# Where the operand and weight tiles of a float32r kernel begin in SBUF

## The chip, the core and the metric

The kernel runs on one core of a Trainium2 chip. The metric is the device time of one execution in microseconds. TensorE (PE in the profile; PEld is its weight load) multiplies; VectorE (DVE) and ScalarE (ACT) do the element work; GpSimd (POOL) and SyncE (SP) start transfers.

## The reference

Attention with a sigmoid in place of the softmax, then two feed-forward networks on its output, all in float32 precision at the end:

```python
scores = matmul(q, k.T) / sqrt(64) - log(448)      # 4 batches, 12 heads, 448 tokens, 64 wide
x = (1 / (1 + exp(-scores))) @ v                   # -> 1792 tokens x 768
h = x @ w_in;  x = maximum(h, 0) ** 2 @ w_out      # 768 -> 2048 -> 768
h = x @ w_in2; out = (h / (1 + exp(-1.702 * h))) @ w_out2
```

The weights come as 8-byte floats and are turned into float32 on the chip.

## The kernel before

**Precision.** TensorE multiplies float32r numbers, which are float32 rounded to fewer bits. For float32 results each operand is split: a high part, rounded to float32r by ScalarE, and a low part, which VectorE makes as the number less its high part. A product is then three matmuls into the same PSUM bank, high times high, high times low, low times high: lines 475, 476 and 477 in `product`. Each streams 448 columns of the operand past 128 × 128 weights, which PEld loads first.

**Tiling.** Each feed-forward matrix product is done in two halves of the tokens (`p`), and each half by a scheme of seven block products instead of eight (P1 to P7 on sums and differences of blocks). That makes 8 stages (`STAGES`) of 56 units (7 products by 8 strips); a unit has 3 chunks of 3 matmuls. 8 × 56 × 9 = 4032 matmuls, run in one fixed order. Attention comes before them, with matmuls of its own: lines 298 (float32r, 64 rows), 317, 332 and 346 (plain float32).

**Tiles that the change touches**, both in the pool `cpool`:

- `T` (line 101): five operand tiles of [128, 2, 3, 448] float32r, 10752 bytes in each partition. Index 0 of the second dimension is the high part, index 1 the low part, and the next index is k, the chunk of 128 rows of the contraction. The class `Operand` picks the tile that has been free longest; ScalarE writes `t[:, 0]` (helper line 153) and VectorE `t[:, 1]` (helper line 156).
- `SL` (line 103): three slots of weights, [128, 2, 2, 384] float32r, 6144 bytes; high and low part, two units, 3 chunks of 128 columns. Unit u uses slot u // 2 % 3. `plan_weights` fills them: SP loads the two units' blocks from DRAM (`scr`) into one of four `LD` tiles, ScalarE writes the high part, VectorE the low part, and TensorE waits for the latter (`lows`).

The pool places its tiles one after the other: X (four of 5376 bytes), T, LD (3072 bytes each), SL, `tmp`, RAW, DEC; after them comes a pool for attention, whose place four tiles for the hidden layer (h) and two of scratch (`sig`) take later. Ahead of all stand the scratch for GpSimd's transfers, 16384 bytes of each partition unless the program says otherwise, and four constants of 32 bytes' room each.

**Weights' way in.** `prep` (32 steps) moves a block of 8-byte floats with POOL's queue into `raw`, decodes it on ScalarE and VectorE into `dec`, makes four sums and differences, and stores blocks and sums with POOL's queue in `scr`. The 96 transfers of these steps are all that POOL starts.

**Order.** `settle` and `run` make a plan before the program is written: every operation is a node with a modelled duration, and a list scheduler orders the nodes of each engine by their latest starts. The plan knows tiles and their users, but no addresses. On the chip each engine runs its list in that order and waits on semaphores.

Of the kernel before, what the change touches and what calls it, by code (L numbers as in the profile page):

```python
# [9 lines left out]
F32R = mybir.dt.float32r  # L10
# [6 lines left out]
B, H, S, D = 4, 12, 448, 64  # L17
DM, DFF = 768, 2048
P = 128
# [10 lines left out]
NK = 3  # L30
NF = 8
W = NK * P
UNITS = 7 * NF
NLOAD = 4
NSLOT = 3
NT = 5
# [42 lines left out]

PACE = (6, 6, 5, 1, 4, 5, 5)  # L80


@with_exitstack
def sigmoid_attention_two_ffn(ctx: ExitStack, tc: tile.TileContext, qk, v, w, outT):
# [3 lines left out]
    nc = tc.nc  # L88
# [9 lines left out]

    cpool = ctx.enter_context(tc.tile_pool(name="cpool", bufs=1))
    X = [[cpool.tile([P, NK, S], F32, name=f"xq{i}{j}") for j in range(2)] for i in range(2)]  # L100
    T = [cpool.tile([P, 2, NK, S], F32R, name=f"t{n}") for n in range(NT)]
    LD = [cpool.tile([P, 2, W], F32, name=f"ld{n}") for n in range(NLOAD)]
    SL = [cpool.tile([P, 2, 2, W], F32R, name=f"s{n}") for n in range(NSLOT)]
    tmp = cpool.tile([P, NK, S], F32, name="tmp")
    RAW = [cpool.tile([P, 4 * W, 2], U32, name=f"raw{n}") for n in range(2)]
    DEC = [cpool.tile([P, 4, W], F32, name=f"dec{n}") for n in range(2)]
# [30 lines left out]
    def act(fn, n, keys=(), after=(), extra=0.0, **kw):  # L137
        return Node("act", fn, 0.115 + extra + 0.833e-3 * n, keys, after, 0.105, **kw)
# [4 lines left out]
    def move(eng, out, in_, size, keys=(), after=(), **kw):  # L143

        def go():
            eng.dma_start(out() if callable(out) else out, in_() if callable(in_) else in_)

        n = Node("sp" if eng is nc.sync else "pool", go, 0.45 if eng is nc.sync else 0.55, keys, after, DMA_US + size / 250e3, **kw)
        n.size = size
        return n  # L150

    def activation(out, in_, fn=AF.Copy, **kw):
        nc.scalar.activation(out, in_, fn, **kw)  # L153
# [9 lines left out]
    def att_order():  # L163
        for u in range(NHP // 2 + 1):
            if u:
                yield from (("V", hp, c) for hp in (2 * u - 2, 2 * u - 1) for c in range(NFULL))
                yield ("VL", u - 1, 0)
            if u < NHP // 2:
                todo = [("S", hp, c) for hp in (2 * u, 2 * u + 1) for c in range(NFULL)]
                todo.insert(0 if u else NFULL, ("SL", u, 0))  # L170
                yield from todo
# [3 lines left out]
    def make_steps():  # L175
        kind = "L"
        us = {"S": SCORES_US, "V": VALUES_US, "VL": LEFT_US, "SL": LEFT_US}
        for key in att_order():
            new = "L" if key[0] in ("VL", "SL") else key[0]
            t = us["V" if key in WHOLE else key[0]]  # L180
# [61 lines left out]
    def load_qk(hp):  # L242
        if hp > 1:
            n = move(nc.sync, RQ[hp % 4], qk[hp], P * 2 * S * 4, (), [pe.get(("SL", (hp - 4) // 2, 0)), split.get(hp - 4)], part=0)
            rq_load[hp] = n, n
# [29 lines left out]
    def next_two():  # L275
        turn[0] += 1
        b = 2 * (turn[0] % 4)
        return b, mem["ps"][:, b : b + 2]
# [28 lines left out]
    def scores_left(u):  # L307
        b, ps = next_two()
        step = pe["SL", u, 0]

# [90 lines left out]
    class Operand:  # L401

        def __init__(self, src, n, keys, first, last):
# [3 lines left out]
            free_t[i] = last  # L407
            self.t = t = T[i]
            keys = [("T", i), *keys]
            act(lambda: activation(t[:, 0, : src().shape[1]], src()), n * S, keys, [units[old]] if old >= 0 else ())  # L410
# [38 lines left out]
    def plan_weights():  # L449
        for q in range(len(STAGES) * UNITS // 2):  # L450
            m, io, _ = STAGES[2 * q // UNITS]
            us = [ORDER[io][(2 * q + i) % UNITS] for i in range(2)]
            t, sl = LD[q % NLOAD], SL[q % NSLOT]
            ld = ("LD", q % NLOAD)
# [414 lines left out]
```

## Time and profile before

| | us |
|---|---|
| median of 2 runs | 951.66 (951.35 to 951.98) |
| the profiled execution: its time | 950.77 |
| its span, first to last instruction | 949.0 |
| TensorE busy | 944.6 (x4949) |
| VectorE busy | 809.3 |
| ScalarE busy | 604.6 |
| GpSimd busy | 53.5 (x100) |

Busy time of TensorE counts matmuls that overlap in its pipeline, so it says that there was always one under way, and not at which rate they went. The step from one start to the next is read from the timeline or from a stretch and the number of its matmuls. Lines 153, 156 and 146 are helpers (`activation`, `tt`, `move`) through which most of ScalarE's and VectorE's work and all transfers of the plan go; their groups are told apart by the tiles' names.

### The profile page before, as it was taken

What the parts mean: (1) busy time and instruction counts of PE and PEld (TensorE: products, weight loads), DVE (VectorE), ACT (ScalarE), POOL (GpSimd) and SP (SyncE); (2) the same over time, 40 slices, a digit from 0 to 9 for tenths busy, and PEclk for the clock granted to TensorE, in tenths of its full rate; (3) what the DMA queues carried; (4) which work ended last, traced back from release to release, by engine and by line L of the source; (5) the groups of instructions that cost most, each with busy time, mean ns of one, the idle gap of its engine ahead of it and who ended that gap; (6) DMA issues with size and microseconds to landing.
All of it is one profiled execution on the core that took longest, in us unless ns stands there. A gap on an engine that the chain in (4) does not pass through costs nothing.

```text
span 949.0 us, 13696 instructions
## 1 busy us (share of the span) xinstructions
PE 944.6 (100%) x4949; PEld 822.8 (87%) x4949; DVE 809.3 (85%) x839; ACT 604.6 (64%) x715; POOL 53.5 (6%) x100
## 2 busy tenths in 40 slices
PE   9999999999999999999999999999999999999998
PEld 4555479999999999999999999999999999999997
DVE  3989986699877999999999987999989999778662
ACT  6788776778868775555464666657684646445551
POOL 0110100000000000000000000000000000000000
PEclk9999999999999999999999999999999999999999
DMA  8899989999886766896567699877975448754341
GB/s 340 301 335 356 335 293 332 324 354 334 290 324 227 250 231 212 317 364 216 161 243 286 202 359 325 312 247 251 351 279 171 133 146 288 261 166 132 115 137 58
DMA packets 98627, 245.75 MB, mean 259 GB/s; under 512 B 10752, under 2 KB 72960, under 8 KB 94464
## 3 DMA queue, kind: packets, MB, share of 16 engines
q1 hardware_dynamic: 84736, 150.51, 46.5%
q0 software_dynamic: 13824, 94.38, 27.2%
q8 instruction: 38, 0.62, 0.3%
q14 instruction: 29, 0.24, 0.1%
HBM read 175.11 MB, written 69.73 MB: 258 GB/s over the span
## 4 chain that ended last, share of the span: by engine, by line
PE 100%; ACT 0%; issue 0%
PE ps L475 29%; PE ps L476 29%; PE ps L477 29%; PE ps L332 6%; PE ps L298 5%; PE ps L346 1%; PE ps L317 1%; PE ps L790 0%; PE ps L293 0%; ACT xq L635 0%; PE ps L471 0%
## 5 line engine op out<-in xcount | busy, mean ns | idle before, releaser
L475 PE MATMUL ps<-t,s 128*128 128x448 f32 x1344 | 490.9, 365 | 0.0
L477 PE MATMUL ps<-t,s 128*128 128x448 f32 x1344 | 490.8, 365 | 0.0
L476 PE MATMUL ps<-t,s 128*128 128x448 f32 x1344 | 490.8, 365 | 0.0
L153 ACT ACTIVATE s<-ld 128x768 fp32r<-128x768 f32 x224 | 189.4, 846 | 249.4 <-PE ps L476 206.6
L477 PEld LDWEIGHTS ps<-t,s 128*128 128x128 f32 x1344 | 252.5, 188 | 19.9
L476 PEld LDWEIGHTS ps<-t,s 128*128 128x128 f32 x1344 | 252.5, 188 | 19.9
L475 PEld LDWEIGHTS ps<-t,s 128*128 128x128 f32 x1344 | 252.5, 188 | 19.9
L156 DVE TENSOR_TENSOR s<-ld,s 128x768 fp32r<-128x768 f32 x224 | 213.6, 954 | 61.7 <-ACT s L153 56.6
L156 DVE TENSOR_TENSOR t<-h,t 128x1344 fp32r<-128x1344 f32 (+1 forms) x72 | 100.4, 1397 | 8.8 <-ACT t L153 8.7
L153 ACT ACTIVATE t<-h 128x1344 fp32r<-128x1344 f32 (+1 forms) x72 | 85.6, 1190 | 4.4 <-DVE h L156 2.9
L153 ACT ACTIVATE h<-ps 128x448 f32<-128x448 f32 x112 | 59.8, 536 | 27.0 <-PE ps L477 26.8
L153 ACT ACTIVATE a<-ps,bias 128x896 f32<-128x896 f32 x72 | 66.1, 1023 | 3.2 <-PE ps L293 3.2
L332 PE MATMUL ps<-a,rv 128*64 128x448 f32 x288 | 56.8, 543 | 0.1
L217 DVE SCALAR_TENSOR_TENSOR dec<-raw,dec 128x1536 uint32<-128x1536 uint32 x32 | 56.2, 1755 | 0.5
L219 DVE SCALAR_TENSOR_TENSOR dec<-raw,dec 128x1536 uint32<-128x1536 uint32 x32 | 56.1, 1753 | 0.3
L153 ACT ACTIVATE dec<-raw 128x1536 f32<-128x1536 f32 x32 | 51.9, 1621 | 0.0
L156 DVE TENSOR_TENSOR h<-h,h 128x1344 f32<-128x1344 f32 (+1 forms) x36 | 50.0, 1397 | 1.0 <-DMA h<-hm 0.8
L153 ACT ACTIVATE h<-h 128x896 f32<-128x896 f32 x48 | 44.9, 945 | 4.8 <-DVE h L156 4.4
L332 PEld LDWEIGHTS ps<-a,rv 128*64 128x64 f32 x288 | 19.6, 137 | 32.4 <-issue 22.6
L213 DVE TENSOR_SCALAR dec<-dec 128x1536 f32<-128x1536 f32 x32 | 30.7, 959 | 15.6 <-ACT dec L153 15.6
L156 DVE TENSOR_TENSOR t<-xq,t 128x1344 fp32r<-128x1344 f32 x24 | 37.2, 1552 | 5.9 <-ACT t L153 5.4
L156 DVE TENSOR_TENSOR h<-ps,h 128x448 f32<-128x448 f32 x64 | 38.8, 619 | 2.8 <-PE ps L477 2.5
(58 smaller groups left out, 616.1 us busy)
## 6 DMA issues: line engine op xcount, KB each, us to landing
ld<-scr SPq DMA_DIRECT2D x448, 192.0 KB, 3.8
raw<-in_w POOLq DMA_DIRECT2D x32, 1536.0 KB, 8.2
scr<-dec POOLq DMA_DIRECT2D x32, 768.0 KB, 5.5
scr<-raw POOLq DMA_DIRECT2D x28, 576.0 KB, 6.2
hm<-h SPq DMA_DIRECT2D x32, 448.0 KB, 5.8
h<-hm SPq DMA_DIRECT2D x16, 672.0 KB, 5.4
rq<-in_qk SPq DMA_DIRECT2D x22, 448.0 KB, 8.2
rv<-in_v SPq DMA_DIRECT2D x12, 448.0 KB, 6.1
```

What stands on the lines that cost most here:

```text
L153: nc.scalar.activation(out, in_, fn, **kw)
L156: nc.vector.tensor_tensor(out=out, in0=in0, in1=in1, op=op)
L213: dve(lambda: nc.vector.tensor_scalar(out=d, in0=d, scalar1=LEAST, scalar2=LARGEST, op0=ALU.max, op1=ALU.min), 4 * W, [dk], each=0.52e-3)
L217: dve(lambda: nc.vector.scalar_tensor_tensor(out=u, in0=raw[:, :, 0], scalar=29, in1=u, op0=ALU.logical_shift_right, op1=ALU.bitwise_or), ...
L219: dve(lambda: nc.vector.scalar_tensor_tensor(out=u, in0=raw[:, :, 1], scalar=0x80000000, in1=u, op0=ALU.bitwise_and, op1=ALU.bitwise_or), ...
L298: nc.tensor.matmul(ps[:, j, :S], kk[rows, keys], qq[rows, QUERIES], start=(i == 0), stop=(i == 2))
L317: nc.tensor.matmul(ps[out, j, :S], r[rows, :LEFT], r[rows, QUERIES], start=True, stop=True)
L332: nc.tensor.matmul(ps[rows, :S], t[:, hp % 2 * NFULL + c, rows], a[:, j], start=(c == 0), stop=False)
L346: nc.tensor.matmul(mem["ps"][out, b + i, :S], t[rows, 2 * NFULL, out], AL[rows, j], start=False, stop=True)
L475: nc.tensor.matmul(o, sh[:, cols], t[:, 0, k], start=start, stop=False, skip_group_check=True)
L476: nc.tensor.matmul(o, sh[:, cols], t[:, 1, k], start=False, stop=False, skip_group_check=True)
L477: nc.tensor.matmul(o, lo[:, cols], t[:, 0, k], start=False, stop=stop, skip_group_check=True)
```

## The change

Each T tile grows from 10752 to 11264 bytes and each SL tile from 6144 to 6656, 512 bytes more, and the part that is used is cut out of the larger tile at an offset: 8, 10, 18, 20 and 24 elements of 4 bytes into T's tiles 0 to 4, and 0, 123 and 106 elements into the three slots. The shape that the rest of the kernel sees is as before. The scratch for GpSimd's transfers is set to 8192 bytes.

```diff
+SKIP_T, SKIP_SL = (8, 10, 18, 20, 24), (0, 123, 106)
...
-    T = [cpool.tile([P, 2, NK, S], F32R, name=f"t{n}") for n in range(NT)]
+    T = []
+    for n, skip in enumerate(SKIP_T):
+        t = cpool.tile([P, 2 * NK * S + P], F32R, name=f"t{n}")
+        T.append(t[:, skip : skip + 2 * NK * S].rearrange("p (a k n) -> p a k n", a=2, k=NK))
     LD = [cpool.tile([P, 2, W], F32, name=f"ld{n}") for n in range(NLOAD)]
-    SL = [cpool.tile([P, 2, 2, W], F32R, name=f"s{n}") for n in range(NSLOT)]
+    SL = []
+    for n, skip in enumerate(SKIP_SL):
+        t = cpool.tile([P, 4 * W + P], F32R, name=f"s{n}")
+        SL.append(t[:, skip : skip + 4 * W].rearrange("p (a i n) -> p a i n", a=2, i=2))
...
-    nc = bacc.Bacc("TRN2", target_bir_lowering=False, num_devices=1)
+    nc = bacc.Bacc("TRN2", target_bir_lowering=False, num_devices=1, dynamic_dma_scratch_size=8192)
```

## Rows read from the trace of the kernel before

**Rows 1.** The page's chain that ended last, shares by engine and line.

```profile
PE 100%; ACT 0%; issue 0%
PE ps L475 29%; PE ps L476 29%; PE ps L477 29%; PE ps L332 6%; PE ps L298 5%; PE ps L346 1%; PE ps L317 1%; PE ps L790 0%; PE ps L293 0%; ACT xq L635 0%; PE ps L471 0%
```

**Rows 2.** Stretch of the 4032 matmuls: its length, then busy us by engine.

```profile
core 0: us, PE busy (x) PEld busy (x) DVE busy (x) ACT busy (x) POOL busy (x), PEclk, DMA share, GB/s
128.22:945.41 817.19, 817.19 (x4032) 757.15 (x4031) 705.94 (x715) 501.66 (x603) 41.91 (x76) 1.00 0.72 248
```

**Rows 3.** Groups by line: names, shapes, count | busy us, mean ns | idle before.

```profile
L475 PE MATMUL ps<-t,s 128*128 128x448 f32 x1344 | 490.9, 365 | 0.0
L477 PE MATMUL ps<-t,s 128*128 128x448 f32 x1344 | 490.8, 365 | 0.0
L476 PE MATMUL ps<-t,s 128*128 128x448 f32 x1344 | 490.8, 365 | 0.0
L475 PEld LDWEIGHTS ps<-t,s 128*128 128x128 f32 x1344 | 252.5, 188 | 19.9
L476 PEld LDWEIGHTS ps<-t,s 128*128 128x128 f32 x1344 | 252.5, 188 | 19.9
L477 PEld LDWEIGHTS ps<-t,s 128*128 128x128 f32 x1344 | 252.5, 188 | 19.9
```

**Rows 4.** Timeline of TensorE from 300 us: start, us, engine, line.

```profile
300.00 0.37 PE L477 MATMUL ps<-t,s 128*128 128x448 f32 x1
300.20 0.36 PE L475 MATMUL ps<-t,s 128*128 128x448 f32 x1
300.41 0.36 PE L476 MATMUL ps<-t,s 128*128 128x448 f32 x1
...
300.21 0.19 PEld L476 LDWEIGHTS ps<-t,s 128*128 128x128 f32 x1
```

**Rows 5.** Timeline of TensorE in attention, from 8.1 us, columns as in rows 4.

```profile
8.14 0.36 PE L298 MATMUL ps<-qh,ql 64*128 64x448 f32 x2
...
9.35 0.37 PE L298 MATMUL ps<-qh,ql 64*128 64x448 f32 x2
```

**Rows 6.** Chain in order of time: start us, us, what.

```profile
15.29 0.75 PE ps L317 x8
```

**Rows 7.** Groups by line, VectorE's writes of s and t.

```profile
L156 DVE TENSOR_TENSOR s<-ld,s 128x768 fp32r<-128x768 f32 x224 | 213.6, 954 | 61.7 <-ACT s L153 56.6 <-DMA ld<-scr 4.0 <-DMA h<-hm 0.3
L156 DVE TENSOR_TENSOR t<-h,t 128x1344 fp32r<-128x1344 f32 x48 | 74.6, 1554 | 8.8 <-ACT t L153 8.7
L156 DVE TENSOR_TENSOR t<-xq,t 128x1344 fp32r<-128x1344 f32 x24 | 37.2, 1552 | 5.9 <-ACT t L153 5.4 <-PE ps L477 0.5
```

**Rows 8.** VectorE from 345 to 450 us: all, then t alone, then s alone.

```profile
345.00:450.00 105.00, 101.63 (x94) 1.00 0.75 262
345.00:450.00 105.00, 30.81 (x22) 1.00 0.75 262
345.00:450.00 105.00, 27.69 (x29) 1.00 0.75 262
```

**Rows 9.** POOL's transfers: count, KB each, median us from issue to landing.

```profile
raw<-in_w POOLq DMA_DIRECT2D x32, 1536.0 KB, 8.2
scr<-dec POOLq DMA_DIRECT2D x32, 768.0 KB, 5.5
scr<-raw POOLq DMA_DIRECT2D x28, 576.0 KB, 6.2
...
scr<-tmp POOLq DMA_DIRECT2D x4, 576.0 KB, 8.7
```

**Rows 10.** Groups on POOL: busy us, mean ns | idle before, and what ended it.

```profile
L146 POOL DMA_DIRECT2D raw<-in_w x32 | 18.1, 566 | 213.8 <-ACT a L153 41.7 <-ACT s L153 39.5 <-DMA scr<-raw 30.8
L146 POOL DMA_DIRECT2D scr<-dec x32 | 17.4, 545 | 395.5 <-DVE dec L156 395.5
L146 POOL DMA_DIRECT2D scr<-raw x28 | 15.4, 550 | 67.9 <-DVE raw L156 67.9
L146 POOL DMA_DIRECT2D scr<-tmp x4 | 2.3, 575 | 3.7 <-DVE tmp L156 3.7
```

**Rows 11.** Waits of SP's queue: us in total, times, longest us.

```profile
SPq L146 <- DVE s L156: 466.7, 210, 9.0
...
SPq L146 <- DMA ld<-scr: 2.0, 2, 1.6
```

## The prediction

> **What bounds the kernel now.** I read the chain of waits first. It belongs to TensorE alone: "PE 100%", and 87% of it is lines 475 to 477, the three matmuls of one product [rows 1]. No wait stands in that chain, so only two things can move the end: the time from one matmul's start to the next, or a new wait that reaches TensorE.
>
> Second, the stretch from the first of these matmuls to the end of the last: 4032 of them in 817.19 us, so one starts every 202.68 ns, with the clock granted in full (1.00, the level of 2.4 GHz) [rows 2]. The first 128 us are attention, the last 4 us the final copies and stores. A matmul streams 448 columns; at one column per cycle of 2.4 GHz that is 448/2.4 = 186.7 ns (at two cycles it would be 373, more than is there). **The excess is 16.0 ns per matmul, 64.5 us in all**, and it is all the time that TensorE's order leaves between this kernel and its own column count.
>
> Third, is that excess even? The timeline shows starts 0.20 us apart whichever line comes next [rows 4], and the grouped rows show 365 ns for each of the three lines and 188 ns for each one's weight load [rows 3]. Here the trace already says something on starting places. All tile sizes of this pool before the change are multiples of 512 bytes, except the four of X, which together are 42 × 512, and those that follow the weights' tiles; so every T and every SL tile starts at the same place within 512. But lines 475 and 477 read the high half of T and line 476 the low half, 5376 bytes = 10.5 × 512 further on: its operand starts half of 512 away from theirs, and the next k (1792 bytes = 3.5 × 512) swaps the two. **A shift of 256 bytes between operand and weights is thus in every second read, and it costs and gains nothing** that the rows show: 365, 365, 365. What they don't show is a shift that is no multiple of 256. Attention's float32r matmuls (L298), whose operand starts 256 bytes further on within 512 than its weights, have the same step: 8.14 to 9.35 in six steps, 202 ns [rows 5].
>
> **The change, part by part.** It adds and removes no instruction, no DMA and no wait; the order on each engine is planned from modelled durations and knows no addresses.
>
> *Operand tiles' start (T).* It touches the read of 4032 matmuls, on the path. The new starts lie 32, 40, 72, 80, 96 bytes off the old place. The trace has no such read. Bounds by the nearest rows: downward the whole excess could go, -64.5 us; upward, a read that came out at the rate of the plain-float32 matmuls of L317 would take 375 ns (four calls of two records each, four records side by side in the four quarters of the array, so two rounds in 0.75 us [rows 6]), +172 ns each; that is a bound, not a case. I take 0, the value of the nearest row, the 256-byte shift [rows 3, 4]. A reason beside it: while a weight load goes on, the operand is read at 1792 bytes per 202.68 ns, 8.8 bytes/ns, and the weights, 512 bytes in at most 188 ns [rows 3], at 2.7 or more. The two reads move at different speeds, so whatever place they start at they run past each other within one matmul; a meeting that costs time would mostly be moved, not removed.
> The Trainium skill ("SBUF — State Buffer", section "Specifications (TRN2)") says that memory lines are of 16 bytes and that each access that crosses to a new line pays a penalty. By that rule the starts at 40 and 72 bytes, 8 past a line, would touch 113 lines and not 112: 202.68/112 = 1.8 ns for two tiles of five, some 2.9 us, so 953.7 us and not 950.8; no run so far shows a start off a line.
>
> *Weights' tiles (SL).* Two of three slots move. Their writes have the work below; their read is the weight load, 188 ns, which starts with the matmul before and has 202.68 - 188 = 14.7 ns left before its own matmul [rows 3, 4]. That cover hides a load longer by up to 8%; past it, each ns is on the path. I take 0; the ends are those of the operand, since the two can only act through the same step.
>
> *Writes into T and SL.* ScalarE writes the high halves, VectorE the low ones (reading the high one too): the VectorE group for s has 224 of 954 ns, those for t 1552 to 1554 ns for 1344 elements [rows 7]. Off the path while VectorE keeps up. The tightest stretch is 345 to 450 us: VectorE 101.63 of 105.00 us, of which t 30.81 and s 27.69 [rows 8]. Its 3.37 us of idle time cover 3.37/58.50 = 5.8% on those instructions. If that cover goes, `lows` come late and the next unit waits. I take 0: same count, shape and element order, and from 768 elements (954 ns) to 1344 (1554) it is 1.04 ns per element and 154 ns besides.
>
> *Everything else in SBUF.* The eight tiles grow by 512 each, 4096 in all, and the scratch shrinks by 8192: all other tiles move by a multiple of 512 and keep their place in it. 0.
>
> *Scratch of 8 KB.* It concerns GpSimd's 96 transfers, each 128 rows [rows 9]. POOL sits idle before them until data are there: VectorE's dec (395.5 us) and raw (67.9 us), or a free buffer (213.8 us, 30.8 of it for an earlier transfer); none is a wait for room that shows [rows 10]. Behind POOL stand the weight loads of SP's queue; its longest wait is for VectorE (466.7 us) and its longest for a load of weights 2.0 us [rows 11]. So 0. From above: had each transfer to wait until the one before it had landed, 5.5 to 8.7 us [rows 9], POOL's idle time before them, 681 us or 7.1 us each, would cover all but 1.6 us of it; that much later SP's loads could come, and the four load tiles, each good for two units, stand before TensorE feels it. Below there is nothing: no such wait is there to win back.
>
> **Sum**: 0 on the profiled execution's 950.77 us (span 949.0 and 1.77 around it); the median of the runs shown is 951.66, 0.1% above. I forecast 951 us, with its own range 944 to 958.
>
> **Rivals.**
> *A, the excess hangs on the two reads starting together (0.26, faster).* For: the excess is no wait and no fixed cost of a matmul, since L317's rounds need 375 ns for 448 columns at two cycles (373.3), 1.7 more and not 16 [rows 6]; so it belongs to the fast stream, and weights are being read in each [rows 4]. All 4032 pairs start now at distances of 0 or 256 within 512, and in the changed kernel none does: the 15 pairs of a T and an SL start 32 to 184 bytes apart. Against: 256 bytes do nothing, and the reads run past each other. If half the excess goes, 4032 × 8.0 = 32 us: 918; all of it, 886. It decides by over 2% from 19/4032 us = 4.7 ns per matmul.
> Another page of the Trainium skill ("TensorE: Matmul & The Clock Gate", "Back-to-back issue gap") gives N/2.4 + 2.5 ns, 189.2 here; if the change reached that, 4032 × 13.5 = 54 us would go: 896. The trace is 13.5 ns above that rule now, and "SBUF — State Buffer", "Who interferes with whom", by which operand and weights have read ports of their own, speaks against this rival.
>
> *B, a read that starts off a grid of 64 bytes is one piece longer (0.12, slower).* Place: the operand's read. The old starts are all on a grid of 128 bytes or finer (the scratch is 16384 bytes, the four constants ahead of the pool 128); of 32, 40, 72, 80, 96 none is a multiple of 64. If the read goes by pieces of 64 bytes, 28 become 29: 202.68/28 = 7.2 ns more, 4032 × 7.2 = 29 us: 980. With pieces of 32 only 40, 72 and 80 are off: 3.6 ns in three tiles of five, 8.8 us, inside 2%. So it decides from 64 bytes up (128: +58 us, 1009). For: the stream is slower than its columns, so its read is near some limit. Against: the smooth 365 ns tell of no pieces [rows 3].
>
> That the change does not do what it says can't be: 11264 and 6656 bytes are 22 and 13 × 512, so the skips are the starts.
>
> **How the numbers follow.** Two per cent, 19 us, is about what a measurement of this kernel can tell from no change; 932 to 970 count as such. The forecast has 0.62, A 0.26, B 0.12. The 0 of the forecast may be off by a part of A or B too small to decide; that is inside. The range goes down to A's middle, as A is likelier than B, and not up to B: 908 to 959 leaves out B (0.12) and A's lower end (0.08). Faster 0.26, same 0.62, slower 0.12.
>
> **What would show it.** The stretch from the first matmul of line 475 to the end: 202 to 203 ns per matmul for the forecast, 195 or less for A, 207 or more for B, and then differing by T tile, with tiles 1 to 3 slowest for finer pieces. VectorE's s at 954 and t at 1552 ns, weight loads at 188. POOL's list without a new wait, SP's without scr. The forecast is wrong if the step changes with no wait behind it, or a wait of line 475 on VectorE's s appears from 345 us on.

## The result, and the profile after

The changed kernel takes 957.49 us (median of 957.18 and 957.81) against 951.66: **0.64% slower**, ratio 1.0064 with a 95% interval of 1.0042 to 1.0086. That is small, inside what the prediction called "the same", but clear of noise, and the prediction had a change of nothing. The profiled execution took 957.81 us, its span 955.3, 6.3 more than before.

First the chain that ended last, of the changed kernel (its lines 483, 484, 485 are 475, 476, 477 of before):

```profile
PE 99%; DMA 0%; ACT 0%; issue 0%
PE ps L483 29%; PE ps L485 29%; PE ps L484 29%; PE ps L340 6%; PE ps L306 5%; PE ps L354 1%; PE ps L325 1%; DMA rq<-in_qk 0%; PE ps L301 0%; ACT xq L643 0%; PE ps L479 0%
```

As in [rows 1] there is no wait among the feed-forward matmuls. So the time went into the step. The stretch of the 4032 matmuls, columns as in [rows 2]:

```profile
core 0: us, PE busy (x) PEld busy (x) DVE busy (x) ACT busy (x) POOL busy (x), PEclk, DMA share, GB/s
128.60:951.80 823.20, 823.20 (x4032) 758.56 (x4030) 706.02 (x715) 501.93 (x603) 41.72 (x76) 1.00 0.71 246
```

823.20/4032 = 204.17 ns, where [rows 2] give 202.68: **+1.5 ns per matmul, 6.0 us, is nearly all of the 6.3.** The clock is 1.00 in both. The groups hide it well, as [rows 3] did: the mean of one matmul goes from 365 to 366 ns, that of a weight load stays at 188.

```profile
L483 PE MATMUL ps<-t,s 128*128 128x448 f32 x1344 | 492.5, 366 | 0.0
L484 PE MATMUL ps<-t,s 128*128 128x448 f32 x1344 | 492.2, 366 | 0.0
L485 PE MATMUL ps<-t,s 128*128 128x448 f32 x1344 | 492.1, 366 | 0.0
L484 PEld LDWEIGHTS ps<-t,s 128*128 128x128 f32 x1344 | 253.3, 188 | 21.5
L485 PEld LDWEIGHTS ps<-t,s 128*128 128x128 f32 x1344 | 252.9, 188 | 21.3
L483 PEld LDWEIGHTS ps<-t,s 128*128 128x128 f32 x1344 | 252.8, 188 | 21.5
```

What is new is that the step is no longer the same for all tiles. Two pieces of the timeline of TensorE in the changed kernel; in the first the operand is in T tile 4 and the weights in slot 1, in the second in tile 1 and slot 2:

```profile
385.64 0.36 PE L485 MATMUL ps<-t,s 128*128 128x448 f32 x1
385.85 0.36 PE L483 MATMUL ps<-t,s 128*128 128x448 f32 x1
...
388.85 0.36 PE L483 MATMUL ps<-t,s 128*128 128x448 f32 x1
389.05 0.36 PE L484 MATMUL ps<-t,s 128*128 128x448 f32 x1
```

```profile
466.71 0.37 PE L483 MATMUL ps<-t,s 128*128 128x448 f32 x1
...
469.81 0.37 PE L483 MATMUL ps<-t,s 128*128 128x448 f32 x1
470.01 0.37 PE L484 MATMUL ps<-t,s 128*128 128x448 f32 x1
```

3.41 us for 17 steps are 201 ns, 3.30 us for 16 steps are 206. In the kernel before every pair had 202.6 to 202.7. The program's order says which tile and which slot each of the 4032 matmuls reads, so all starts of the trace can be sorted by the T tile of a matmul and the slot of the weights that are loaded beside it (those of the next matmul). Mean step in ns, 230 to 303 matmuls in each field:

```
changed kernel       slot 0 (+0)   slot 1 (+492)   slot 2 (+424 bytes)
T tile 0 (+32)          205.4          204.2           204.5
T tile 1 (+40)          203.1          205.3           206.0
T tile 2 (+72)          205.6          202.9           204.2
T tile 3 (+80)          203.1          205.9           204.0
T tile 4 (+96)          205.1          200.7           203.1
```

No row and no column is good or bad by itself: tile 4 is among the slow ones beside slot 0 and the best of all beside slot 1. That made the theory to be tested: **the pair decides**. The rest is as it was. VectorE's group for s takes 955 ns (954 in [rows 7]):

```profile
L164 DVE TENSOR_TENSOR s<-ld,s 128x768 fp32r<-128x768 f32 x224 | 213.9, 955 | 65.5 <-ACT s L161 57.2 <-DMA ld<-scr 4.7 <-DMA h<-hm 2.7
```

In the tightest stretch, VectorE's work in all, then t, then s, as in [rows 8]:

```profile
345.00:450.00 105.00, 101.10 (x93) 1.00 0.76 265
345.00:450.00 105.00, 29.29 (x21) 1.00 0.76 265
345.00:450.00 105.00, 27.64 (x29) 1.00 0.76 265
```

POOL, the engine of the smaller scratch, shows no wait for room; its two larger groups of stores wait for VectorE, as in [rows 10]:

```profile
L154 POOL DMA_DIRECT2D scr<-dec x32 | 17.4, 544 | 406.2 <-DVE dec L164 392.8 <-DVE raw L164 13.4
L154 POOL DMA_DIRECT2D scr<-raw x28 | 15.4, 549 | 67.7 <-DVE raw L164 67.7
```

### The profile page after: what moved, and what is told of

It is laid out like the page before. It is cut to its first block, busy times and chain, and to the rows that moved or that the text cites. A ratio compares the mean times of both kernels' runs of the same rounds, so it can differ in the third digit from the quotient of the medians.

```text
span 955.3 us, 13696 instructions
## 1 busy us (share of the span) xinstructions
PE 950.9 (100%) x4949; PEld 824.4 (86%) x4949; DVE 809.6 (85%) x839; ACT 605.0 (63%) x715; POOL 53.2 (6%) x100
## 2 busy tenths in 40 slices
DMA packets 98627, 245.75 MB, mean 257 GB/s; under 512 B 10752, under 2 KB 72960, under 8 KB 94464
## 4 chain that ended last, share of the span: by engine, by line
PE 99%; DMA 0%; ACT 0%; issue 0%
PE ps L483 29%; PE ps L485 29%; PE ps L484 29%; PE ps L340 6%; PE ps L306 5%; PE ps L354 1%; PE ps L325 1%; DMA rq<-in_qk 0%; PE ps L301 0%; ACT xq L643 0%; PE ps L479 0%
```

## Experiments

Theory PAIR: the step of a matmul depends on where its operand's read starts and where the read of the weights loaded beside it starts, the two together. Rival OWN START: each read that starts off a grid costs by itself. Rival SCRATCH: the 6 us come from the smaller scratch or from the moved places of other tiles. The sweeps tell starts in elements of 4 bytes, a for the operand and b for the weights, from a multiple of 512 bytes; the kernel's tiles have 32 elements (128 bytes) more, on both sides.

**e1_pads: the change without its skips.**

```diff
-SKIP_T, SKIP_SL = (8, 10, 18, 20, 24), (0, 123, 106)
+SKIP_T, SKIP_SL = (0, 0, 0, 0, 0), (0, 0, 0)
```

> All skips are 0: the larger tiles, the shifted places of everything else and the 8 KB scratch of the change are kept, the starting places are those of before. The step between two matmul starts was 202.68 ns before and is 204.20 ns after the change. Theory PAIR (the step depends on where the operand's read and the read of the weights loaded beside it start, relative to one another and to a grid): 202.7 ns and about 951.7 us, a ratio of 1.000 to the kernel before. Theory OWN START (each read off a grid costs by itself, T's or SL's): the same, 951.7. Rival SCRATCH (the scratch or the moved places of other tiles made the 6 us): about 957.5.

951.41 us (median of 12), ratio 1.000 (0.9991 to 1.0009). SCRATCH is out: tiles 512 bytes larger, all other tiles moved, and half the scratch cost nothing.

**e2_pair: the best pair of the table, everywhere.**

```diff
-SKIP_T, SKIP_SL = (8, 10, 18, 20, 24), (0, 123, 106)
+SKIP_T, SKIP_SL = (24, 24, 24, 24, 24), (123, 123, 123)
```

> All five T tiles at 96 bytes and all three SL slots at 492, the one pair that stood out in the trace of the changed kernel: T tile 4 with slot 1 had a mean step of 200.6 ns in 285 matmuls, where the other 14 pairs had 202.9 to 206.0. Theory PAIR: 200.6 to 200.7 ns everywhere, (200.65 - 202.68) x 4032 = -8.2 us, about 943.5. Theory OWN START, by the means of tile 4 (202.84 over all slots) and slot 1 (203.57 over all tiles) against 204.20 over all: 204.20 - 1.36 - 0.63 = 202.2 ns, -1.9 us, about 949.8.

940.77 us, ratio 0.9888 (0.9874 to 0.9903). The stretch of the 4032 matmuls:

```profile
128.80:935.30 806.50, 806.50 (x4032) 757.89 (x4031) 704.78 (x715) 501.45 (x603) 42.30 (x76) 1.00 0.73 251
```

806.50/4032 = 200.02 ns, and 199.9 to 200.1 in every field of the table. OWN START, which allowed 949.8, falls; PAIR was right but for 2.7 us: the pair's mean in the changed kernel, 200.65, held some longer steps. Of its 25 passages of eight matmuls or more in a row, 21 ran at 200.0 ns after their first two steps and four at 201.6 to 204.8.

**e3_t_only: T's skips alone.**

```diff
-SKIP_T, SKIP_SL = (8, 10, 18, 20, 24), (0, 123, 106)
+SKIP_T, SKIP_SL = (8, 10, 18, 20, 24), (0, 0, 0)
```

> T's five skips as in the change, SL's all 0. Theory PAIR, from the steps that each T tile had with slot 0 in the changed kernel (205.43, 203.05, 205.62, 203.08, 205.15): mean 204.5, +1.8 ns or 7 us, about 958.9, with tiles 1 and 3 about 2.4 ns below the others. Theory OWN START with T at fault: the means of the tiles over all slots, 204.74, 204.75, 204.20, 204.32, 202.84, so about 957.7 and tile 4 the fastest; with SL at fault: 951.7.

959.28 us, ratio 1.0085 (1.0072 to 1.0098).

```profile
128.16:953.78 825.62, 825.62 (x4032) 759.68 (x4031) 706.16 (x715) 502.05 (x603) 41.63 (x76) 1.00 0.71 245
```

204.77 ns. By tile, averaged over the slots, 205.8, 203.2, 206.0, 203.4, 205.4: tiles 1 and 3 are about 2 ns or more below the others and tile 4 is not the fastest, as PAIR had it from the column of slot 0.

**e4_sl_only: SL's skips alone.**

```diff
-SKIP_T, SKIP_SL = (8, 10, 18, 20, 24), (0, 123, 106)
+SKIP_T, SKIP_SL = (0, 0, 0, 0, 0), (0, 123, 106)
```

> SL's three skips as in the change, T's all 0. Theory PAIR, from the sweep of matmuls alone at the same places (a 0 with b 0: 202.7, b 123: 204.7, b 106: 206.7): mean 204.7 ns, +2.0 x 4032 = 8 us, about 959.6, by slot 202.7, 204.7 and 206.7. Theory OWN START, by which T's part and SL's part add up: the whole change costs 6.0 us and T alone cost 7.8, so SL alone gives -1.8 us, 949.7.

964.71 us, ratio 1.0143 (1.0126 to 1.016): 13.6 us more than the 951.16 beside it, where T's part alone cost 7.8 and both together 5.8. The parts do not add up, and not even nearly. OWN START, which had 949.7, falls again. But PAIR missed by 5 us as well. Slots 1 and 2 came out as it said, 204.6 to 204.7 and 206.8 to 206.9; slot 0, which stands exactly as in the kernel before, took 206.1 to 206.4 and not 202.7. The timeline of TensorE in this run, first in unit 0 and 1 (slot 0, nothing else used so far), then when slot 0 comes round again:

```profile
129.20 0.37 PE L483 MATMUL ps<-t,s 128*128 128x448 f32 x1
...
131.64 0.36 PE L483 MATMUL ps<-t,s 128*128 128x448 f32 x1
...
139.86 0.37 PE L484 MATMUL ps<-t,s 128*128 128x448 f32 x1
...
142.96 0.37 PE L484 MATMUL ps<-t,s 128*128 128x448 f32 x1
```

2.44 us for 12 steps, 203 ns; then 3.10 us for 15 steps, 207. Same slot, same starts, another step. That asked for m4 below.

**m1_sweep: matmuls alone, over the starts.** Its core:

```python
for a, b in pairs:                       # 4 sweeps of 128 pairs
    for i in range(12):
        nc.tensor.matmul(o, Wt[:, b : b + 128], M[:, a : a + 448], start=i == 0, stop=i == 11)
```

> Not the kernel: matmuls of 128 x 128 weights and 448 float32r columns alone, with no other engine at work, in runs of 12 with the same starts; a = start of the operand and b = start of the weights in elements of 4 bytes, from places that are multiples of 512 bytes. Four sweeps: a 0 to 127 with b 0; b 0 to 127 with a 0; a = b 0 to 127; a 0 to 127 with b 5. Theory PAIR: the step varies by several ns along the first and second sweep, as in the changed kernel (200.6 to 206), and (0, 0) gives 202.7. If only the distance a - b counts, the third sweep is flat at 202.7 and the fourth is the first one shifted by 5. Theory OWN START: the third varies like the first, and the fourth equals the first but for a constant. If the variation in the changed kernel came from other engines' traffic, all four are flat.

Step in ns, worked out from the starts of matmuls 3 to 12 of each run; the first sweep (b = 0), and one period of the third (a = b):

```
a =  0..7   202.7  207.2  206.4  200.0  201.0  206.7  205.0  200.0
a =  8..15  204.4  205.0  202.3  201.6  202.9  206.7  204.4  200.0
a = 16..23  200.0  206.8  206.7  200.0  203.4  206.7  204.7  204.6
a = 24..31  205.4  207.0  206.7  200.2  205.3  206.7  205.8  200.0
a = 32..39  203.8  210.2  207.9  200.0  206.7  205.1  205.2  205.7
a = 40..47  201.9  208.9  206.9  203.3  204.3  206.7  200.0  200.0
a = 48..55  202.2  205.0  206.8  203.1  204.1  207.2  206.9  206.7
a = 56..63  203.2  207.0  206.4  199.8  202.6  206.7  201.3  200.1
a = b = 8..15   202.8  200.0  203.7  200.0  201.9  201.2  205.3  200.6
```

(0, 0) gives the 202.7 of the kernel before, with no other engine at work. The values of a = 64 to 127 repeat those of 0 to 63 within 0.1: **the period is 64 elements, 256 bytes.** In the third sweep the values repeat every 8 elements: a common shift by 32 bytes changes nothing, a shorter one does. Two runs are exceptions: (1, 1) and (2, 2), among the first of the sweep, took 208.0 and 206.7 ns, where their repeats took 200.0 and 203.7. So not the distance alone counts, but the distance and the place within 32 bytes. OWN START fails here too, as the fourth sweep (b = 5) is not the first one with a constant added: 207.3, 203.1, 206.0, 200.0, 204.4, 202.1, 200.0, 200.1 for a = 0 to 7 (here too the first two do not repeat: 200.0 and 205.7 at a = 64 and 65).

**e5_pad64: a faster kernel without skips.**

```diff
+    SL = [cpool.tile([P, 2, 2, W], F32R, name=f"s{n}") for n in range(NSLOT)]
+    cpool.tile([P, 16], F32, name="pad")
     T = [cpool.tile([P, 2, NK, S], F32R, name=f"t{n}") for n in range(NT)]
     LD = [cpool.tile([P, 2, W], F32, name=f"ld{n}") for n in range(NLOAD)]
-    SL = [cpool.tile([P, 2, 2, W], F32R, name=f"s{n}") for n in range(NSLOT)]
```

> The kernel before with no skips and the 16 KB scratch; only SL stands ahead of T in the pool and one tile of 64 bytes between them, so that every operand's read starts 64 bytes further on than every weights' read within 256. Theory PAIR with the period of 256 bytes that the sweep showed (a 16, b 0: 200.0 ns): 200.0 ns, -2.68 x 4032 = -10.8 us, about 940.7, as fast as the 96 and 492 of all tiles. Rival: the fast pair needs starts off a grid (40 bytes off 64 for the weights), and a plain pad gives 202.7 and 951.5.

940.53 us, ratio 0.9889 (0.9874 to 0.9904), the scratch at its 16 KB:

```profile
128.45:934.96 806.51, 806.51 (x4033) 755.58 (x4032) 704.55 (x715) 501.28 (x603) 41.79 (x76) 1.00 0.73 251
```

200.0 ns. This beats both kernels, by 10.6 us on the one before (951.16 beside it) and by 17.0 on the changed one, with one tile of 64 bytes and SL's line moved ahead of T's. The pair has a distance a - b of 16 elements, both starts on multiples of 32 bytes, so the rival falls: the fast step needs no start off that grid.

**m2_map: all pairs.** The same loop over d = a - b from 0 to 63 for b from 0 to 7.

> Not the kernel: the sweep of matmuls alone for 512 pairs, distance d = a - b from 0 to 63 elements for each b from 0 to 7, runs of 12. Theory PAIR with the two periods of the first sweep (256 bytes in the distance, 32 bytes in a common shift): these 512 are all cases there are; the mean of the 15 pairs of the changed kernel comes out at 204.2 within 0.3, no pair lies under 200.0, and the mean of the map tells what a random choice costs (first sweep: 203 to 204, so +1 ns and some +4 us). Rival, that the step also depends on the pair before: the 15 pairs give another mean than 204.2.

The 512 steps lie between 200.0 (199.8 by the grain of the time stamps) and 217.3, mean 204.1; a fifth of them are at 200.0, the middle one is 203.9, and a tenth are over 207.4. A third are under 202.4, six in ten over 203. Read at the pairs of the kernels, weighted by how often each is used, the map gives 202.67 for before (measured 202.67), 204.07 for the change (204.18), 200.0 for e2 and e5 (200.0), 204.46 for T's skips alone (204.75) and 204.62 for SL's alone (205.91). Four of these five means are met within 0.3; the fifth is e4.

That the mean of the changed kernel is met is partly luck, since the map's own mean is 204.1. The single fields of its table are missed by up to 3.1 ns (tile 4 beside slot 2: 200.0 in the map, 203.1 in the kernel). And of the first 64 pairs of m1's second sweep, which by the two periods stand in the map as well, 17 differ from it by more than 1 ns, most of all (0, 27): 200.0 there, 217.3 here. So the two starts alone do not settle the step of every pair. These two runs can't tell whether the pair before counts or a period that does not hold for all pairs.

**m3_shapes: where the rest comes from.** The same loop in runs of 24, for three pairs, five widths and two weights' widths, then bfloat16.

> Not the kernel: matmuls alone at three pairs (a, b) = (0, 0), (16, 0), (33, 0), whose steps are 202.7, 200.0 and about 208 ns at 448 columns, now with 448, 512, 384, 256 and 128 columns and with weights of 128 and of 64 columns, runs of 24; then bfloat16, 128 starts of the operand in steps of 2 bytes, runs of 12. Where does the rest of 13.3 ns over 448/2.4 come from, that no pair takes away? Read of the weights beside it: with 64 columns of weights it halves, 193.3 at (16, 0), and it does not change with the columns streamed. Stream of the operand itself: 512 columns 228.6, 256 columns 114.3, 64 columns of weights change nothing. Fixed per matmul: N/2.4 + 13.3 at every N. In bfloat16 half the bytes are read: a flat sweep if the reads meet only at the full rate of 4 bytes a column.

Step less columns/2.4, ns, from the starts of matmuls 5 to 24:

```
columns, weights   (0, 0)  (16, 0)  (33, 0)
512, 128            14.7    20.0     22.6
512,  64            16.9    15.1     21.5
448, 128            15.8    13.2     26.5
448,  64            15.5    14.7     23.0
384, 128            13.9    13.4     18.5
384,  64            13.2    13.4     19.2
256, 128            13.3    11.1     16.1
256,  64             6.7    10.1     13.6
128, 128            58.4    58.1     58.4
128,  64             6.7     8.8      9.5
bfloat16, 448 columns, 128 starts: step 189.0 to 190.0
```

With half the weights the rest does not halve at 448 columns, so it is not the length of the weights' read; it is not in proportion to the columns and not fixed either. All three guesses fail, and what the 13.3 ns are that no pair takes away stays open. Three things do follow. The good pair at one width need not be good at another: at 512 columns and 128 of weights (16, 0) is slower than (0, 0), 233.3 against 228.0 ns. At 128 columns with 128 of weights all three pairs take 111.5 to 111.7 ns: there the pair makes no difference. And bfloat16, with half the bytes for a column, is flat over these 128 starts of the operand: as far as this was tried, the effect belongs to float32r.

**m4_history: does the past count?**

```python
for i in range(6 + 24):
    a, b = first if i < 6 else target    # 64 pairs `first`, targets (0, 0) and (16, 0)
    nc.tensor.matmul(o, Wt[:, b : b + 128], M[:, a : a + 448], start=i == 0, stop=i == 29)
```

> Not the kernel: matmuls alone; 6 at one of 64 other pairs, then 24 at the pair (0, 0), the one of the kernel before; then the same 64 ahead of 24 at (16, 0). In the run with SL's skips alone, slot 0 stood at (0, 0) and took 206.1 to 206.4 ns a step, not 202.7, though its first 16 steps, before any other slot was used, took 202.7. Theory PAIR WITH A PAST: (0, 0) has two steps that keep themselves up, and which of them it is depends on what ran ahead: some of the 64 runs end at 202.7 and some at 206.7, each constant over its last 18 steps; (16, 0) ends at 200.0 in all. Rival, that the change of slots itself costs: the steps are long just after the change of pair and come back to 202.7 within a few, in all 64.

At (0, 0) the last ten starts of each run give 207 ns in 31 of 64 runs and 202 to 203 in 33; nothing came back. At (16, 0) it is 200.0 in all 64. Two runs at (0, 0), steps in ns from the first of the 24 on:

```
after (8, 0)     203 203 199 207 203 202 203 199 206 203 202 203 199 207 202
after (11, 1)    200 201 207 207 206 207 207 206 207 207 206 207 207 206 207
```

**So the pair of the kernel before has two steps that keep themselves up, 202.7 and 206.7, and which of them a run took went with what ran ahead of it.** These are the runs of one execution. That fits e4: its slot 0 took 203 ns on its first turn and, once past the first three steps, 206.6 to 206.7 on every one of its 74 later turns, each behind slot 2 (whose own pair is not among the 64). The changed kernel's trace shows it too. Tile 4 beside slot 2 came 22 times for eight matmuls or more in a row: six times at 200.0 ns, eight times at 203.3 to 203.6 and eight times at 206.7 to 206.8 (first two steps left out). The fields of its table are means over such passages, so the pair decides together with its past.

The whole kernel can run in the longer step. In e1 all starts are those of the kernel before; its profiled execution took 968.36 us, with no wait of TensorE in the stretch:

```profile
128.93:962.28 833.35, 833.35 (x4032) 756.62 (x4031) 706.37 (x715) 501.85 (x603) 40.97 (x76) 1.00 0.70 243
```

833.35/4032 = 206.7 ns, with the clock at 1.00, and even from the third matmul on. One more of e1's 12 executions (967.87 us) and one of the 17 of the kernel before beside them (967.78) took about as long, without a trace. The program was the same each time, so its order alone does not choose between the two steps; what does is not shown.

**e6_worst: a slow pair everywhere.**

```diff
-SKIP_T, SKIP_SL = (8, 10, 18, 20, 24), (0, 123, 106)
+SKIP_T, SKIP_SL = (33, 33, 33, 33, 33), (0, 0, 0)
```

> All T tiles 132 bytes (33 elements) further on, SL's skips 0: one of the slow pairs of the sweep, 210.2 ns. Theory PAIR: 210.2 ns everywhere, +7.5 x 4032 = 30 us, about 982. If the sweep, which had no other engine at work, does not carry over to the kernel: 203 to 206 ns, 953 to 965.

995.19 us, ratio 1.0462 (1.0432 to 1.0493):

```profile
128.69:988.85 860.16, 860.16 (x4032) 774.73 (x4031) 708.17 (x715) 502.54 (x603) 41.22 (x76) 1.00 0.68 235
```

860.16/4032 = 213.3 ns, not 210.2. The sweep's run of 12 was too short for this pair: in m3's run of 24 the steps settle at 213 to 214 after the fifth, and 213.3 would have said 994. The effect carries over to the kernel in full; it is no matter of other engines' traffic.

## Why the prediction was wrong

**The step that failed** is the first one of the sum: "I take 0, the value of the nearest row, the 256-byte shift". The rows were read rightly, a shift by 256 bytes does nothing, but 256 bytes are the whole period (m1), so this row was the one shift that could not show the effect. The terms for T and for SL, both put at 0, were together +1.5 ns × 4032 = 6.0 us, and the change measured +5.8. The prediction even wrote that the rows don't show "a shift that is no multiple of 256", and took their value nevertheless. The two terms can't be priced apart either: T's part alone cost 7.8 us, SL's alone 13.6.

**The reason beside it**, that two reads of different speed run past each other so that a meeting is "mostly moved, not removed", was half true. No pair removes the excess: of 16.0 ns the best takes 2.7. But the pairs of the map differ by up to 17 ns, so where the reads start does change what a meeting costs.

**Rival A** (the excess hangs on the two reads together) had the right cause and the wrong sign for these offsets: the pair does decide, with what ran before it, and the full gain that is there, 10.7 us, is a third of its middle value. The change picked 15 pairs, one of them near the floor, the other fourteen slower than before; with a map whose mean is 204.1, 204.2 is what a blind choice of 15 pairs gets. Its numbers, 918 and 886, took for granted that half or all of the excess can go. **Rival B** (one piece more for a read off a grid of 64 bytes) had the right sign and the wrong cause: with T's skips alone all tiles would have been slower alike by 7.2 ns; they were by 0.5 to 3.3, and a = 16, which is on the grid, is faster than a = 0.

**The Trainium skill's** rule of 16-byte lines ("SBUF — State Buffer", "Specifications (TRN2)") does not carry this: beside slot 0, tiles 1 and 2, which start off a line, took 203.1 and 205.6 ns, tiles 0, 3 and 4, on a line, 205.4, 203.1 and 205.1. And by "Who interferes with whom" on that page operand and weights have read ports of their own. In m1, with no other engine at work, moving the weights alone took the step from 202.7 to 204.7 (b = 123) and 206.7 ns (b = 106), so the measurement decides otherwise for float32r: the two reads are not independent in time. How they get in each other's way is not shown.

**What held, and what did by luck.** No wait for weights appears, and their loads stay at 188 ns, in e2 and e5 too. But the cover of 14.7 ns was misread: in m3 matmuls of 128 columns follow one another every 111.7 ns at (0, 0) with loads of 188 ns each, so a load longer than the step need not hold the next matmul up. Writes into T and SL: 955 ns for s, and no wait of TensorE for VectorE in the stretch. Everything else in SBUF and the scratch: 0 (e1). 957.49 lies in the forecast's own range of 944 to 958, at its upper end, by luck: nothing in the sum stood for the 5.8 us, and either part of the change alone (959.28 and 964.71) would have been outside.

The prediction also misread two totals of [rows 11], on which nothing hung: 466.7 us are 210 waits, the longest 9.0, and 2.0 us are two, the longest 1.6. And 2% was far more than a measurement of this kernel needs to tell a change: the interval here is 0.42% to 0.86%.

## What to carry to other kernels

Before a row is used as the nearest one for a shift, ask which shifts it could show at all: tiles that all begin at the same place within 256 bytes had kept every other shift out of view, and the same step over 4032 matmuls looked like proof. Where float32r matmuls follow one another without a wait, the place of the weights' tile against the operand's is worth a sweep at the kernel's own column count; a pad of 64 bytes gave 1.1% here, while matmuls alone in bfloat16 showed nothing to gain (189.0 to 190.0 ns at every start of the operand). Look for a pair that has one step only: (16, 0) came to 200.0 ns in all 64 runs of m4, and e5's four executions lie within 0.9 us, where equal starts gave 951 us or 968. Parts of such a change are not to be tried one by one and added: T alone +7.8 us, SL alone +13.6, both +5.8.

## What the runs showed of the hardware

At 448 float32r columns 184 of the 512 pairs of m2 hold an even step (the last eight agree within 1 ns): 111 at 200.0 ns, 55 at 206.7 and 18 at other values from 203.2 to 213.4; e6 ran at an even 213.3. Other pairs show patterns of unequal steps that repeat, such as 199, 207, 203, 202, 203, 202 or the like at (0, 0), and a mean can come about both ways: in m3 (16, 0) reached its 200 by 197, 202, 201. One pair can have two steps or more, and in m4 the choice went with the pair before. Why float32r at its best needs 200.0 ns and bfloat16 189 for the same 448 columns (448/2.4 = 186.7) was not settled: half as many weights columns do not shorten it (199.8 with 128 and 201.4 with 64 at (16, 0)).
